# Attention segments with merged value tiles, a quarter of a normalisation on ScalarE, and scores between value projections

## The chip, the cores and the metric

One core of a Trainium2 chip. The metric is device time of one execution in microseconds; lower is better. TensorE (PE) does matmuls into PSUM, VectorE (DVE), ScalarE (ACT) and GpSimd (POOL) do the rest, and SyncE (SP) issues most DMAs. The kernel is one unrolled program; nothing is decided at run time.

## The reference

A transformer block on 2048 tokens of width 640. Only its first part matters here: a recurrent attention, 64 segments of 32 tokens, 32 heads of 128, with 8 memory tokens that each segment hands to the next.

```python
for s in range(n_seg):                      # 64
    xs = x[:, s * seg_len:(s + 1) * seg_len, :].copy()
    h = jnp.concatenate([mem, xs], axis=1)  # 8 + 32 tokens
    q = jnp.einsum('btd,dhe->bhte', h, Wq)  # k and v alike
    scores = jnp.einsum('bhqe,bhke->bhqk', q, k) * scale
    scores = jnp.where(mask[None, None], scores, -1000000000.0)
    p = _softmax(scores, axis=-1)
    o = jnp.einsum('bhqk,bhke->bhqe', p, v)
    o = jnp.einsum('bhte,hed->btd', o, Wo)
    mem = o[:, :M, :].copy()
    outs.append(o[:, M:, :])
```

x is layer-normalised before it. Behind it come a residual, a second layer norm and a gated ReLU feed-forward (640 to 1728 to 640), with a residual again.

## The kernel before, in words

All weights of the attention lie in SBUF. The program is a list of operations, written in one order; `_Graph` works out which semaphores each must wait for, and every engine runs its own operations in the order of the list. PSUM has eight banks, named `BQ` (0 and 1), `T0`, `T1` (2, 3) and `P0` to `P3` (4 to 7).

A segment's 40 tokens are split: 32 rows of `act_r` hold the memory and 24 tokens, and the last 8 tokens of four segments share one tile, `act_e`, whose keys, queries and values (`Ke`, `Qe`, `Ve`) are made once for four segments, in the group before. So each segment has two sets of keys and values: its own (`Ko`, `Vp`, index a = 0) and the shared ones (`Ke`, `Ve`, a = 1).

One turn of the loop over `s` does, on TensorE, in this order:

1. K projection of `act_r` in two halves of 16 heads (`project`, L374: five chunks of the width, four matmuls each side by side on column groups of 32, 512 columns). ScalarE evicts each half (`to_tok`, L395), VectorE transposes it in blocks of 32 (`flip`, L390) into `Ko`.
2. `pv_x(s-1)`: probabilities times values for the 32 new queries of the segment before, into banks 0 to 3, in tiles of 32 rows by 32 columns. `norm_x` divides by the row sum (a column of ones in the value tiles): one reciprocal (L648) and two products over 128x512 (L651) on VectorE, into `ox`; `flip_ox` (L535) transposes `ox` into `oT`.
3. Q projection in two halves, evicted and flipped as K, into `Qo`.
4. V projection half 0, `scores(s,0)`, V projection half 1, `scores(s,1)`. A call of `scores` is 32 matmuls (L460) with 40 columns. The values are evicted by ScalarE into `Vp` (two buffers, by the parity of s).
5. `pv_mem(s,0)`, a filler, `pv_mem(s,1)`, a filler: the 8 memory queries. Before each come `exp_mem` (ScalarE, into `Pm`) and `mask_mem` (VectorE, into `Pbd`); behind each `norm_mem` and `flip_mem` into `oT`. The fillers are parts of the shared projections (`extra_units`) or of the output projection of the shared tokens (`woe_pass`, L615).
6. `wo_split` (L572) and `wo_pass` (L555), the output projection. Its memory rows become, through `fold_split` and `to_act_split`, the first rows of the next `act_r`; the other rows go to DRAM from `wtok`.
7. The rest of the filler, while that runs; then the next segment.

`exp_x` and `mask_x` make the probabilities `Px` that the next turn's `pv_x` uses. SP also loads and transposes x for the segments to come (once in four segments).

Of the kernel before, what the change touches and what calls it, by code (L numbers as in the profile page):

```python
# [163 lines left out]
def build_kernel(nc, A_x, A_mem0, A_Wq, A_Wk, A_Wv, A_Wo, A_seg_len, B_W_gate, B_W_up, B_W_down, out):  # L164
# [57 lines left out]
    mca = ar.alloc("mca", [128, 5, SEG], BF16)  # L222
    act_r = [ar.alloc(f"act_r{i}", [128, 4, DC, 32], BF16) for i in range(2)]
    act_e = [ar.alloc(f"act_e{i}", [128, DC, 32], BF16) for i in range(2)]
    tok = [ar.alloc(f"tok{i}", [128, 512], BF16) for i in range(4)]
# [5 lines left out]
    Vp = [ar.alloc(f"Vp{i}", [128, 8, VW], BF16) for i in range(2)]  # L231
# [8 lines left out]
    ox = ar.alloc("ox", [128, 4, 2, Dh], BF16)  # L240
    wtok = [ar.alloc(f"wtok{i}", [128, DC, 32], BF16) for i in range(2)]
# [36 lines left out]
    for i in (1, 0):  # L278
        add("pool", lambda p, i=i: p.memset(wtok[i][:], 0.0), w=[("wtok", i)])
# [4 lines left out]
    for i in range(2):  # L284
# [3 lines left out]
        add("pool", lambda p, i=i: p.memset(ap(Vp[i], Dh, [[VW, 8], [1, VW - Dh]]), 1.0), w=[("Vp1", i)])  # L288
# [4 lines left out]
    for g in range(4):  # L293
        for n in range(5):
            sl = mca[32 * g:32 * g + 32, n, :]
            add("pool", lambda p, sl=sl, n=n: p.affine_select(sl, sl, [[1, SEG]], ALU.is_ge, 0.0,
                                                              base=M if n == 0 else M * (n - 1) - RID,
                                                              channel_multiplier=-1), r=[("mca",)], w=[("mca",)])
            if n > 1:
                add("pool", lambda p, sl=sl, n=n: p.affine_select(sl, sl, [[0, SEG]], ALU.is_ge, 0.0,  # L300
                                                                  base=-M * (n - 1), channel_multiplier=1),
                    r=[("mca",)], w=[("mca",)])
    add("pool", lambda p: p.memset(mbd[:], 0.0), w=[("mbd",)])
    for g in range(4):
        add("pool", lambda p, g=g: p.memset(mbd[32 * g:32 * g + 32, :, 8 * g:8 * g + 8], BIG), r=[("mbd",)], w=[("mbd",)])
# [73 lines left out]

    def to_tok(b, t, eng):  # L380
        copy_op(eng, tok[t][:, :], bank(b), [B(b)], [("tok", t)])
# [7 lines left out]
    def flip(t, dst, i, keys):  # L389
        add("dve", lambda v: v.transpose(dst[:, 16 * i:16 * i + 16, 0:32], tok[t][:, :].rearrange("p (h f) -> p h f", f=32)),  # L390
            r=[("tok", t)], w=keys)
# [58 lines left out]
    def scores(s, hf):  # L450
# [3 lines left out]
        def f(pe):  # L454
            for k in range(4 * hf, 4 * hf + 4):
                for a in range(2):
                    for g in range(4):
                        h = head(k, g)
                        o = 160 * a + 40 * (k % 4)
                        i = pe.matmul(bank((P0, P1)[hf])[32 * g:32 * g + 32, o:o + 40],  # L460
# [13 lines left out]
    def exp_mem(s, hf):  # L474
        _, j = place(s)
        add("act", lambda a: a.activation(ap(Pm, 32 * hf, [[64, 2], [8, 4], [1, 8]]), s_view(hf, 0, M), ACTF.Exp,
                                          scale=SCALE), r=[B((P0, P1)[hf])], w=[("Pm", hf)])

    def mask_mem(s, hf):
        _, j = place(s)  # L480
        for i in (1, 0):
            add("dve", lambda v, i=i: v.tensor_tensor(ap(Pbd, 256 * i + 128 * hf, [[32, 4], [8, 4], [1, 8]]),
                                                      ap(Pm, 64 * i + 32 * hf, [[8, 4], [0, 4], [1, 8]]),
                                                      ap(mbd, 32 * (1 + j) * i, [[0, 4], [8, 4], [1, 8]]), ALU.min),
# [7 lines left out]
    def mask_x(s):  # L492
# [3 lines left out]
                                             ap(mca, 0, [[32 * (1 + j), 2], [0, 8], [1, 32]]), ALU.min),  # L496
            r=[("Px", 0), ("Px", 1), ("mca",)], w=[("Px", 0), ("Px", 1)])

    def v_of(s, a):
        par, p = s % 2, place(s)[0]  # L500
        if a == 0:
            return Vp[par], [("Vp", par, i) for i in range(2)] + [("Vp1", par)]
        return Ve[p], [("Ve", p, i) for i in range(2)] + [("Ve1", p)]

    def pv_mem(s, hf):
# [10 lines left out]
        (vp, e), par = place(s), s % 2  # L516
        add("pe", f, r=[("Pbd", a, hf) for a in range(2)] + [("Ve", vp, hf), ("Ve1", vp), ("Vp", par, hf), ("Vp1", par)],
            w=[B(bk)])

    def norm_mem(s, hf):  # L520
# [3 lines left out]
        add("act", lambda a: a.activation(om[:, hf, :], src[:, 0:128], ACTF.Copy, scale=rm[:, hf:hf + 1]),  # L524
            r=[B(bk), ("rm", hf)], w=[("om", hf)])
# [6 lines left out]
    def flip_ox(s, halves=(0, 1)):  # L532
        p = (s + 1) % 2
        for kh in halves:
            add("dve", lambda v, kh=kh: v.transpose(ap(oT[p], 160 * kh + M, [[320, 4], [40, 4], [1, 32]]),  # L535
                                                       ap(ox, 128 * kh, [[256, 4], [1, 4], [4, 32]])),
                r=[("ox", kh)], w=[("oT", p, "x", kh)])
# [90 lines left out]

    def pv_x(s, b0):
        (t0, k0), (t1, k1) = v_of(s, 0), v_of(s, 1)  # L630

        def f(pe):
            for kh in range(2):
                for a in range(2):
                    for c in range(4):
                        k = 4 * kh + c
                        for g in range(4):
                            i = pe.matmul(bank(b0 + g)[32 * c:32 * c + 32, 129 * kh:129 * kh + 129],  # L638
                                          Px[32 * g:32 * g + 32, 256 * a + 32 * k:256 * a + 32 * k + 32],
                                          (t0, t1)[a][32 * g:32 * g + 32, k, 0:129], start=(a == 0), stop=(a == 1),  # L640
                                          skip_group_check=True, tile_position=(32 * g, 32 * c))
            return i
        add("pe", f, r=[("Px", 0), ("Px", 1)] + k0 + k1, w=[B(b0 + g) for g in range(4)])
# [254 lines left out]
    for s in range(1, NSEG):  # L898
# [16 lines left out]
        if s > 0:  # L915
# [24 lines left out]
            if s > 1:  # L940
                flip_ox(s - 1, (0,))
# [301 lines left out]
```

## Time and profile before

| | |
|---|---|
| median of 3 runs | 1027.08 us (1026.67 to 1027.17) |
| the profiled execution | 1026.84 us |
| its span | 1025.1 us |
| PE, PEld, DVE, ACT, POOL busy | 97%, 55%, 70%, 49%, 16% |
| granted TensorE clock | 0.998 |

A line of the page or the trace gives the line of the kernel, engine, operation and tiles; `x` is a count. In a timeline the first two numbers are start and length in microseconds from the start of the span, and a bracket at the end gives the engine's idle time before it and what ended that. PEld is TensorE's weight load, which overlaps its matmuls. A matmul's length holds its way through the array, so starts, not lengths, show the pace.

### The profile page before, as it was taken

To read this page: it belongs to the slowest core of one execution; us is meant where nothing else is said; L and a number is where in the kernel's file an instruction comes from. 1 tells how busy PE (TensorE), PEld (TensorE's weight loads), DVE (VectorE), ACT (ScalarE), POOL (GpSimd) and SP (SyncE) were. 2 spreads that over 40 slices of the span, in tenths; PEclk is the share of its full clock that TensorE was granted. 3 is DMA by queue.
4 is the path that set the end of the run, shared out by engine and by line. 5 is a ranking of instruction groups with operands and counts; after the bars stand their busy time and mean duration, and the time that the engine had idled before them with its cause. 6 is when DMAs were issued, how large, how long until landed. Compare 5 with 4: busy or idle time off the path is not lost.

```text
span 1025.1 us, 57915 instructions
## 1 busy us (share of the span) xinstructions
PE 994.6 (97%) x27201; PEld 559.5 (55%) x26104; DVE 716.0 (70%) x1796; ACT 501.5 (49%) x1262; POOL 168.8 (16%) x402
## 2 busy tenths in 40 slices
PE   4789999999999999999999999999999999999998
PEld 1255656565656565656565566656565554444443
DVE  2558787878778787888888778787777765355332
ACT  1345555555555555565556555555555542121220
POOL 6020202120202020222222222121210010000000
PEclk9999999999999999999999999999999999999999
DMA  9920100010001001111212111000000048413100
GB/s 372 416 68 6 21 7 21 7 22 7 21 7 22 7 21 12 29 18 23 46 27 32 28 32 22 20 8 16 9 6 8 8 114 242 130 27 90 27 14 26
DMA packets 58531, 52.23 MB, mean 51 GB/s; under 512 B 37840, under 2 KB 55216, under 8 KB 56368
## 3 DMA queue, kind: packets, MB, share of 16 engines
q1 hardware_dynamic: 56160, 47.23, 16.7%
q8 instruction: 208, 3.41, 1.4%
q10 hardware_dynamic: 2128, 1.31, 0.5%
q14 instruction: 35, 0.29, 0.1%
HBM read 37.04 MB, written 6.55 MB: 43 GB/s over the span
## 4 chain that ended last, share of the span: by engine, by line
PE 93%; SPq 3%; DMA 2%; issue 0%; DVE 0%; ACT 0%; DVEq 0%; ACTq 0%
PE ps L374 47%; PE ps L817 11%; PE ps L555 7%; PE ps L572 7%; PE ps L357 6%; PE ps L638 4%; PE ps L615 4%; SPq L320 3%; PE ps L1049 3%; PE ps L460 3%; DMA Wo<-in_A_Wo_dram 2%; PE ps L513 2%; PE ps L830 0%; PE ps L1061 0%; DVE TBf L595 0%
## 5 line engine op out<-in xcount | busy, mean ns | idle before, releaser
L374 PE MATMUL ps<-W,act_r 128*32 128x512 bf16 x7580 | 448.3, 381 | 2.1 <-DVE act_r L596 1.4
L374 PEld LDWEIGHTS ps<-W,act_r 128*32 128x32 bf16 x7580 | 190.6, 96 | 201.5 <-DVE act_r L596 31.2
L395 ACT ACTIVATE tok<-ps 128x512 bf16<-128x512 f32 x324 | 189.0, 597 | 163.5 <-PE ps L374 134.4
L374 PE MATMUL ps<-W,act_e 128*32 128x512 bf16 x1224 | 121.2, 383 | 7.5 <-DMA W<-in_A_Wv_dram 4.0
L468 POOL COPY Qo<-Qe 128x256 bf16<-128x256 bf16 x64 | 31.8, 497 | 547.4 <-DVE oT L529 524.4
L390 DVE STREAM_TRANSPOSE Ko<-tok 128x512 bf16<-128x512 bf16 x128 | 89.6, 701 | 40.0 <-ACT tok L395 36.9
L395 ACT ACTIVATE Vp<-ps 128x512 bf16<-128x512 f32 x127 | 75.8, 597 | 69.2 <-PE ps L374 69.2
L390 DVE STREAM_TRANSPOSE Qo<-tok 128x512 bf16<-128x512 bf16 x126 | 88.9, 706 | 14.1 <-ACT tok L395 14.1
L535 DVE STREAM_TRANSPOSE oT<-ox 128x512 bf16<-128x512 bf16 x128 | 87.8, 687 | 0.0
L357 PE MATMUL ps<-W,act_e 128*32 128x512 bf16 x856 | 87.7, 385 | 0.0
L555 PE MATMUL ps<-Wo,oT 128*32 128x160 bf16 x4032 | 83.3, 233 | 1.0 <-issue 0.6
L651 DVE TENSOR_TENSOR ox<-ps,rx 128x512 bf16<-128x512 f32 x128 | 82.5, 687 | 2.2
L572 PE MATMUL ps<-Wo,oT 128*32 128x320 bf16 x2016 | 81.2, 299 | 0.0
L555 PEld LDWEIGHTS ps<-Wo,oT 128*32 128x32 bf16 x4032 | 75.7, 97 | 5.8 <-DMA Wo<-in_A_Wo_dram 1.3
L585 ACT ACTIVATE SA<-TA 64x40 f32<-64x40 f32 x126 | 29.5, 234 | 84.9 <-DVE TA L583 84.2
L845 ACT ACTIVATE g<-ps 128x512 bf16<-128x512 f32 x52 | 30.1, 593 | 82.8 <-PE ps L817 82.8
L817 PE MATMUL ps<-xn2T,Wu 128*128 128x512 bf16 x260 | 64.6, 379 | 0.0
L846 DVE TENSOR_TENSOR hT<-g,ps 128x512 bf16<-128x512 bf16 x52 | 35.8, 688 | 40.5 <-PE ps L817 40.1
L572 PEld LDWEIGHTS ps<-Wo,oT 128*32 128x32 bf16 x2016 | 56.4, 96 | 13.8 <-issue 1.1
L374 PEld LDWEIGHTS ps<-W,act_e 128*32 128x32 bf16 x1224 | 37.1, 97 | 47.8 <-issue 34.8
L817 PE MATMUL ps<-xn2T,Wg 128*128 128x512 bf16 x246 | 61.6, 379 | 1.5 <-issue 1.1
L529 DVE STREAM_TRANSPOSE oT<-om 128x128 bf16<-128x128 bf16 x126 | 39.2, 311 | 29.4 <-ACT om L524 28.1
(109 smaller groups left out, 1359.1 us busy)
## 6 DMA issues: line engine op xcount, KB each, us to landing
W<-in_A_Wk_dram SPq DMA_DIRECT2D x5, 1024.0 KB
W<-in_A_Wq_dram SPq DMA_DIRECT2D x5, 1024.0 KB
W<-in_A_Wv_dram SPq DMA_DIRECT2D x5, 1024.0 KB
Wo<-in_A_Wo_dram SPq DMA_DIRECT2D x8, 640.0 KB
attn_d<-wtok SPq DMA_DIRECT2D x248, 7.5 KB
xt<-in_A_x_dram SPq DMA_DIRECT2D x16, 160.0 KB
at<-attn_d SPq DMA_DIRECT2D x16, 160.0 KB
out_dram<-osb SPq DMA_DIRECT2D x15, 160.0 KB
```

The costliest lines, as they stand in the source:

```text
L357: return pe.add_instruction(mybir.InstMatmult(name=nc.get_next_instruction_name(), engine=mybir.EngineType.PE, ins=[pe.lower_ap(rhs), pe.l ...
L374: ins = pe.matmul(*a, start=(c == 0), stop=(c == DC - 1), skip_group_check=True)
L390: add("dve", lambda v: v.transpose(dst[:, 16 * i:16 * i + 16, 0:32], tok[t][:, :].rearrange("p (h f) -> p h f", f=32)), r=[("tok", t)], w= ...
L395: add("act", lambda a: a.activation(dst, src, ACTF.Copy), r=r, w=w)
L529: add("dve", lambda v: v.transpose(ap(oT[par], 160 * hf, [[40, 4], [320, 4], [1, 8]]), ap(om, 128 * hf, [[1, 4], [4, 32]])), r=[("om", hf) ...
L535: add("dve", lambda v, kh=kh: v.transpose(ap(oT[p], 160 * kh + M, [[320, 4], [40, 4], [1, 32]]), ap(ox, 128 * kh, [[256, 4], [1, 4], [4, 3 ...
L555: i = pe.matmul(bank(bk)[32 * gg:32 * gg + 32, 0:160], src[:, hb, 0:32], w[:, gg], start=(hb == CH[16 * halves[0]]), stop=(hb == CH[-1]), ...
L572: i = pe.matmul(bank(bk)[32 * q:32 * q + 32, 0:320], src[:, hb, 0:32], w, start=(n == 0), stop=(n == 7), skip_group_check=True)
L615: ins = pe.matmul(bank(bk)[32 * q:32 * q + 32, 0:320], src[:, hb, 0:32], w[:, 2 * (q % 2):2 * (q % 2) + 2], start=(i == 0), stop=(i == 15) ...
L638: i = pe.matmul(bank(b0 + g)[32 * c:32 * c + 32, 129 * kh:129 * kh + 129], Px[32 * g:32 * g + 32, 256 * a + 32 * k:256 * a + 32 * k + 32], ...
L651: add("dve", lambda v, kh=kh: v.tensor_tensor(ox[:, :, kh, :], src[:, :, kh, 0:128], ap(rx, kh, [[2, 4], [0, 128]]), ALU.mult), r=[B(b0 + ...
L817: ins = pe.matmul(bank(bk), w[:, c, lo:lo + 128], xn2T[par][:, c, :], start=(c == 0), stop=(c == DC - 1))
```

## The change

- The scores of the two key sets are written so that partitions 64u to 64u + 63 hold, for one head, the probabilities of both sets. To match, the shared values are projected with neighbouring head groups swapped, and `merge_v` copies `Vp` and `Ve` by DMA from SP into two merged value tiles `VM`: four copies of 32 partitions per segment, and four more once in four segments. `pv_x` then needs 32 matmuls on tiles of 64 rows by 32 columns instead of 64 on 32 by 32, without accumulation. `Vp` and `wtok` lose a buffer; `ox` shares memory with two of the `tok` tiles (`tox`).
- `norm_x` does the reciprocal and the first half of the product on VectorE. `norm_x_late`, after the eviction and flip of the first Q half, does the rest: a quarter on VectorE, a quarter on ScalarE in two pieces.
- Scores come in runs of 16 matmuls: after four of the five chunks of a value half, and after the fifth.
- `exp_mem(s,0)` and `exp_mem(s,1)` stand ahead of the evictions of the value halves. `norm_mem(s,0)` scales on VectorE instead of ScalarE.
- `pv_x(0)` moves from the start into the turn s = 1.

```diff
+    tox = ar.alloc("tox", [128, 4, 2, Dh], BF16)
+    tok = [tox[:].rearrange("p g k d -> p (g k d)")[:, 512 * i:512 * i + 512] for i in range(2)]
...
-    Vp = [ar.alloc(f"Vp{i}", [128, 8, VW], BF16) for i in range(2)]
+    Vp = ar.alloc("Vp", [128, 8, VW], BF16)
+    VM = [ar.alloc(f"VM{i}", [128, 8, VW], BF16) for i in range(2)]
...
     def project(act, akeys, j, halves, banks, chunks=range(5)):
+        swap = 1 if j == 2 and akeys[0][0] == "acte" else 0
...
-                        w = (W[:, j, c, o + 512 * g:o + 512 * g + 512] if j == 2 else
+                        w = (W[:, j, c, o + 512 * (g ^ swap):o + 512 * (g ^ swap) + 512] if j == 2 else
...
-    def scores(s, hf):
+    def scores(s, hf, ks=range(4)):
...
-            for k in range(4 * hf, 4 * hf + 4):
+            for k in [4 * hf + n for n in ks]:
                 for a in range(2):
                     for g in range(4):
                         h = head(k, g)
-                        o = 160 * a + 40 * (k % 4)
-                        i = pe.matmul(bank((P0, P1)[hf])[32 * g:32 * g + 32, o:o + 40],
+                        o, q = 160 * (g % 2) + 40 * (k % 4), 32 * (g ^ a)
+                        i = pe.matmul(bank((P0, P1)[hf])[q:q + 32, o:o + 40],
...
-        add("act", lambda a: a.activation(om[:, hf, :], src[:, 0:128], ACTF.Copy, scale=rm[:, hf:hf + 1]),
-            r=[B(bk), ("rm", hf)], w=[("om", hf)])
+        if hf:
+            add("act", lambda a: a.activation(om[:, hf, :], src[:, 0:128], ACTF.Copy, scale=rm[:, hf:hf + 1]),
+                r=[B(bk), ("rm", hf)], w=[("om", hf)])
+        else:
+            add("dve", lambda v: v.tensor_scalar(om[:, hf, :], src[:, 0:128], rm[:, hf:hf + 1], None, ALU.mult),
+                r=[B(bk), ("rm", hf)], w=[("om", hf)])
...
+    def merge_v(s, a):
+        (t, ks), flat = v_of(s, a), "p k d -> p (k d)"
+        for r in range(2):
+            for g in range(4):
+                if g % 2 == r ^ a:
+                    dma(VM[r][32 * g:32 * g + 32].rearrange(flat), t[32 * g:32 * g + 32].rearrange(flat), r=ks,
+                        w=[("VM", r, g)])
+
     def pv_x(s, b0):
...
-                for a in range(2):
+                for r in range(2):
                     for c in range(4):
                         k = 4 * kh + c
-                        for g in range(4):
-                            i = pe.matmul(bank(b0 + g)[32 * c:32 * c + 32, 129 * kh:129 * kh + 129],
-                                          Px[32 * g:32 * g + 32, 256 * a + 32 * k:256 * a + 32 * k + 32],
-                                          (t0, t1)[a][32 * g:32 * g + 32, k, 0:129], start=(a == 0), stop=(a == 1),
-                                          skip_group_check=True, tile_position=(32 * g, 32 * c))
+                        for u in range(2):
+                            i = pe.matmul(bank(b0 + 2 * u + r)[32 * c:32 * c + 32, 129 * kh:129 * kh + 129],
+                                          Px[64 * u:64 * u + 64, 256 * r + 32 * k:256 * r + 32 * k + 32],
+                                          VM[r][64 * u:64 * u + 64, k, 0:129], start=True, stop=True,
+                                          skip_group_check=True, tile_position=(64 * u, 32 * c))
...
+    def norm_x_late(b0):
+        src = ps[:, b0 * 512 + 1024:b0 * 512 + 2048].rearrange("p (g r) -> p g r", r=512)[:, :, 129:257]
+        add("dve", lambda v: v.tensor_tensor(tox[:, 2:4, 1, :], src, ap(rx, 5, [[2, 2], [0, 128]]), ALU.mult),
+            r=[B(b0 + 2), B(b0 + 3), ("rx",)], w=[("ox", 1, 1)])
+        for g in range(2):
+            add("act", lambda a, g=g: a.activation(tox[:, g, 1, :], bank(b0 + g)[:, 129:257], ACTF.Copy,
+                                                   scale=rx[:, 2 * g + 1:2 * g + 2]),
+                r=[B(b0 + g), ("rx",)], w=[("ox", 1, 0)])
...
-            if s > 1:
-                pv_x(s - 1, 0)
-                norm_x(0)
+            pv_x(s - 1, 0)
+            norm_x(0)
+            if s % 4 == 2:
+                merge_v(s, 1)
             if not last:
                 for i in range(2):
                     project(a, ks, 0, (i,), ((P0, P1)[i],))
                     to_tok((P0, P1)[i], 2 + i, "act")
                     flip(2 + i, Qo, i, [("Qo", i)])
-            if s > 1:
+                    if i == 0:
+                        norm_x_late(0)
+                        flip_ox(s - 1, (0,))
...
-            project(a, ks, 2, (0,), (P2,))
-            to_v(P2, Vp[par], 0, ("Vp", par), "act")
+            project(a, ks, 2, (0,), (P2,), range(4))
+            scores(s, 0, (0, 1))
+            project(a, ks, 2, (0,), (P2,), (4,))
+            scores(s, 0, (2, 3))
+            if not last:
+                exp_mem(s, 0)
+                mask_mem(s, 0)
+            to_v(P2, Vp, 0, ("Vp",), "act")
...
-        exp_mem(s, 0)
-        mask_mem(s, 0)
-        if s > 0:
-            if s > 1:
-                flip_ox(s - 1, (1,))
-            to_v(P3, Vp[par], 1, ("Vp", par), "act")
+        project(a, ks, 2, (1,), (P3,), range(4))
+        scores(s, 1, (0, 1))
+        project(a, ks, 2, (1,), (P3,), (4,))
+        scores(s, 1, (2, 3))
+        flip_ox(s - 1, (1,))
...
         exp_mem(s, 1)
+        to_v(P3, Vp, 1, ("Vp",), "act")
+        merge_v(s, 0)
         pv_mem(s, 0)
```

The masks (`mbd`, `mca`) and the layouts of `Pm` and `Pbd` follow the new places of the scores.

More of the change, by code (lines that the diff above doesn't have):

```diff
@@ L239, in build_kernel @@
     rx = ar.alloc("rx", [128, 8], F32)
-    ox = ar.alloc("ox", [128, 4, 2, Dh], BF16)
-    wtok = [ar.alloc(f"wtok{i}", [128, DC, 32], BF16) for i in range(2)]
+    wtok = ar.alloc("wtok", [128, DC, 32], BF16)
     TBf = ar.alloc("TBf", [128, DC, 32], F32)
@@ L275, in B @@
         return ("B", n)
-    for i in (1, 0):
-        add("pool", lambda p, i=i: p.memset(wtok[i][:], 0.0), w=[("wtok", i)])
+    add("pool", lambda p: p.memset(wtok[:], 0.0), w=[("wtok",)])
     add("pool", lambda p: p.memset(ident[:], 1.0), w=[("ident",)])
@@ L378, in project, with tok_keys @@
         add("pe", f, r=list(akeys) + [("W", j, c) for c in chunks], w=[B(b) for b in banks] + [("Wdone", j)])
+    def tok_keys(t):
+        return [("tok", t)] + [("ox", kh, t) for kh in range(2) if t < 2]
     def to_tok(b, t, eng):
-        copy_op(eng, tok[t][:, :], bank(b), [B(b)], [("tok", t)])
+        copy_op(eng, tok[t][:, :], bank(b), [B(b)], tok_keys(t))
     def to_v(b, t, i, key, eng):
@@ L515, in f @@
             return i
-        (vp, e), par = place(s), s % 2
-        add("pe", f, r=[("Pbd", a, hf) for a in range(2)] + [("Ve", vp, hf), ("Ve1", vp), ("Vp", par, hf), ("Vp1", par)],
+        vp = place(s)[0]
+        add("pe", f, r=[("Pbd", a, hf) for a in range(2)] + [("Ve", vp, hf), ("Ve1", vp), ("Vp", hf), ("Vp1",)],
             w=[B(bk)])
@@ L709, in build_kernel @@
     w0 = bank(T1)[:, 0:160]
-    copy_op("dve", w0, wtok[1][:].rearrange("p c t -> p (c t)"), [("wtok", 1)] + [("wtok0", g) for g in range(4)],
+    copy_op("dve", w0, wtok[:].rearrange("p c t -> p (c t)"), [("wtok",)] + [("wtok0", g) for g in range(4)],
             [B(T1), ("w0",)])
@@ L872, in build_kernel @@
     pv_mem(0, 1)
-    pv_x(0, P0)
+    for a in (1, 0):
+        merge_v(0, a)
     for hf in range(2):
@@ L963, in build_kernel @@
             gate_up(0, 0)
-        scores(s, 1)
-        if last:
+            scores(s, 1)
             exp_x(s, 1)
@@ L1132, in build_kernel @@
     norm_x(P0)
+    norm_x_late(P0)
     flip_ox(s)
```

89 lines of the change are left out of this document (45 added, 44 removed).

## The prediction

> **What bounds it now.** I read the page first, then the list of TensorE's waits, then TensorE's timeline through one segment, then VectorE's and ScalarE's over the same stretch, and last the records of DMA packets. The page:
>
> ```profile
> PE 994.6 (97%) x27201; PEld 559.5 (55%) x26104; DVE 716.0 (70%) x1796; ACT 501.5 (49%) x1262; POOL 168.8 (16%) x402
> PEclk9999999999999999999999999999999999999999
> PE 93%; SPq 3%; DMA 2%; issue 0%; DVE 0%; ACT 0%; DVEq 0%; ACTq 0%
> ```
>
> TensorE is busy 97% at full clock and carries 93% of the chain that ends last. Its list of waits:
>
> ```profile
> PE ps L374 <- DVE act_r L596: 1.4, 2, 0.8
> PE ps L513 <- DVE Pbd L482: 0.8, 1, 0.8
> ```
>
> These are the largest that lie inside the 64 segments (the longer ones are in the start). So only a shorter TensorE stream can shorten this kernel, and only if nothing it waits for becomes late. One segment takes 12.40 us (three in four; the fourth, with the load of x, 12.5 to 13.0). Where is TensorE busy but badly used?
>
> ```profile
> 406.72 0.82 PE L374 MATMUL ps<-W,act_r 128*32 128x512 bf16 x12
> 407.47 0.28 PE L638 MATMUL ps<-Vp,Px 32*32 32x129 bf16 x16
> 407.54 0.28 PE L638 MATMUL ps<-Ve,Px 32*32 32x129 bf16 x16
> 407.72 0.35 PE L638 MATMUL ps<-Vp,Px 32*32 32x129 bf16 x16
> 407.86 0.35 PE L638 MATMUL ps<-Ve,Px 32*32 32x129 bf16 x16
> 408.13 0.61 PE L374 MATMUL ps<-W,act_r 128*32 128x512 bf16 x8
> ```
>
> This is `pv_x`. Four 512-column matmuls side by side take 0.2165 us in the projections (60 in 3.25 us), so 129 columns stream in 0.054 us, and four rounds of 16 tiles could take 0.22 us. The rounds start at 0, 0.07, 0.25 and 0.39 us, and the next projection at 0.665. The first two rounds are 64 instructions (weight loads and matmuls); from there each pair comes 8.3 ns after the last, the pace at which instructions arrive, not stream. After the last matmul's start another 0.157 us pass before the projection.
>
> ```profile
> 411.38 0.19 PE L460 MATMUL ps<-Qo,Ko 128*32 128x40 bf16 x4
> 411.41 0.19 PE L460 MATMUL ps<-Qo,Ke 128*32 128x40 bf16 x4
> ...
> 411.54 0.19 PE L460 MATMUL ps<-Qo,Ko 128*32 128x40 bf16 x4
> 411.57 0.23 PE L460 MATMUL ps<-Qo,Ke 128*32 128x40 bf16 x4
> 411.63 1.28 PE L374 MATMUL ps<-W,act_r 128*32 128x512 bf16 x20
> ```
>
> A half of the scores: groups of four start 25.5 ns apart while instructions are at hand, and the last groups are spread out; 32 matmuls cost 0.25 us.
>
> **Part by part.** *pv_x, 32 matmuls on 64-row tiles instead of 64.* Its 64 instructions are what the fast stretch held. Entry and exit stay (still two changes of tile shape). Four rounds of 8 tiles: the last matmul starts at 0.03 + 3 x (0.054 to 0.071) = 0.19 to 0.24, plus 0.157 out: 0.35 to 0.40 against 0.665, a gain of 0.27 to 0.32; I take 0.29. The loop and the tail have 63 that were on the path: -18.3 us. No row has a 64-row tile; if the two row halves did not run side by side, eight rounds would leave a gain of about 0.04, the other bound. The Trainium skill ("TensorEngine Tiling (Array Packing)", Tiling Modes) lists 64x32 as eight independent tiles, which would be the first bound; no run here shows it.
>
> *pv_x(0) moves* from the start, where it lay under the load of Wo (the chain has 20.13 us of that from 35.40), into segment 1: about +0.5 us.
>
> *Scores in runs of 16.* Two halves now cost 0.25 each, with 0.007 more in the projection behind. A run of 16 is 32 instructions, so it never runs dry: four steps of 25.5 ns, 0.10 us, four runs per segment. But the order of the column groups is now 0,1,2,3,1,0,3,2, so a group returns after three matmuls instead of four; at 3.5 ns between matmuls this adds up to 0.014 per run. Gain 0.05 to 0.10, and nothing if each added entry costs another 0.015; I take 0.07 x 62 = -4.3 us.
>
> *Merge DMAs.* Four per segment (eight in one of four) on SP, 66 KB each, 32 rows of 2080 bytes. They wait for the second value eviction, which ends about 0.9 us after the start of `pv_mem(s,0)`, and are issued at about 0.4 us each (four stores of `wtok` took 1.51), done by 2.6. The 160 KB load of x began to move 1.0 us after its issue and its last row landed, behind an instruction fetch, at 3.0. So they land 4 to 5.6 us after `pv_mem(s,0)`; `pv_x` comes 6.9 us after it. Queued behind them on SP are the `wtok` stores, whose next writer comes a segment later, and behind the four that wait for `pv_x` only the next merge, 5 us on; so they cost nothing. If they landed 2 us later still, that cover would be gone and each further microsecond would cost 62.
>
> *Their packets against instruction fetches.* TensorE's program comes in 16384-byte blocks, 0.92 to 1.0 us each usually, up to 1.8 while x is loading; then the `wo` passes sometimes stop without a semaphore (0.47 us at 167.2, 0.56 at 565.8). Those passes use 128 instructions in 1.1 us. The merge puts about two rows per engine and DMA there, against eight for x. Bounds 0 and 0.5 us per segment; only blocks fetched in the 1.1 us before those passes matter, so I take the low end, +1 us in all. The Trainium skill ("Runtime: NRT & Kernel Launch", Instruction fetch mechanics) says that TensorE holds 2048 instructions and that crossing a block is mostly hidden. By that rule this term would be 0 and the total 1 us lower; the two stops speak against it.
>
> *Waits on TensorE.* `pv_x` now waits for four DMA semaphores. A semaphore instruction on TensorE takes 0.051 us, two follow 0.11 apart (929.32), and matmuls already queued went on at their 0.136 step beside them; here the 64 instructions ahead are 1.7 us of projection. So 0; if they were exposed, 0.22 x 62 = 14 us. `pv_mem(s,0)` now waits for ScalarE too: the first value eviction, after `exp_mem(s,0)`, ends about 0.3 us before it is wanted.
>
> *VectorE and ScalarE.* Here the cover is thin.
>
> ```profile
> 408.22 0.71 DVE L390 STREAM_TRANSPOSE Ko<-tok 128x512 bf16<-128x512 bf16 x1 [0.37 <-ACT tok L395]
> 408.86 0.17 DVE L648 RECIPROCAL rx<-ps 128x8 f32<-128x8 f32 x1
> 409.06 1.29 DVE L651 TENSOR_TENSOR ox<-ps,rx 128x512 bf16<-128x512 f32 x2
> 410.26 0.70 DVE L390 STREAM_TRANSPOSE Qo<-tok 128x512 bf16<-128x512 bf16 x1
> 411.16 0.71 DVE L390 STREAM_TRANSPOSE Qo<-tok 128x512 bf16<-128x512 bf16 x1 [0.19 <-ACT tok L395]
> ```
>
> Count from the first load of `pv_x` (407.47). The reciprocal stays at 1.39, the first half of the normalisation at 1.59; the first Qo flip follows at 2.28 (its eviction comes 0.29 earlier than now). `norm_x_late` on VectorE, 256 elements from PSUM: 0.32 us for 160 (L602) and 0.69 for 512 bound it, about 0.42 on their line; it starts at 2.91. `flip_ox` at 3.25, and the second Qo flip, formerly third, at 3.85, done at 4.56, visible to TensorE at 4.61. TensorE wants it for the second half of the scores at 0.375 + 2.165 (Q) + 0.866 + 0.105 + 0.2165 + 0.105 + 0.866 = 4.70. It is 0.09 us early, where before it was 0.8 early. ScalarE's two pieces (0.37 each, L524's shape) fit between the two Qo evictions, which leave 0.48 idle plus the earlier start. Behind it, `exp_mem(s,1)` now precedes the value eviction (0.27 earlier), `om(0)` on VectorE (128 elements, about 0.29) replaces a ScalarE step and its semaphore, and Pbd's second half comes 1.08 after `pv_mem(s,0)`, as now; TensorE asks for it at 1.13. So two covers under 0.1 us: I add +1 us for segments that miss them.
>
> **Sum.** -18.3 + 0.5 - 4.3 + 1 + 1 = -20.1. The profiled execution took 1026.84 (span 1025.10 and 1.74 around it), 0.24 below the median of 1027.08: 1006.7, and 1007.0 for the median.
>
> **Rivals.** (1) *VectorE becomes the bound.* If `norm_x_late` takes a full-size 0.69 instead of 0.42, the second Qo flip is 0.18 late in every segment: 62 x 0.18 = 11, 1017 with the 1 us above taken out. For it: 9 to 10.3 us busy of 12.4 per segment, with no idle from 1.39 on. Against: the operand is half as large. (2) *64-row tiles run one half at a time*: +0.25 x 63 = 16, 1023. For it: no row; against: 4 x 4 tiles of 32 rows do run together. (3) *The other side: fetches behind the merge.* If every segment stops for the 0.47 us seen at 167.2, 62 x 0.47 = 29, 1035 with the 1 us taken out. It decides from 0.34 us per segment, where the gain is gone. For it: the merge falls into the `wo` passes each time; against: 1/4 of x's rows per DMA. (4) *The change doesn't do its work faster*, since exit and entry, not arrival, set 0.665: excluded by the 8.3 ns pace of the last 32 pairs. (5) *More than I take*: rounds at 0.054 and runs at 0.10 throughout, no stops: 63 x 0.03 + 62 x 0.03 + 2 = 6 less, 1001.
>
> **Numbers.** Forecast 0.60 (1003 to 1012), more than taken 0.12 (998 to 1003), VectorE 0.13 (1012 to 1020), half tiles 0.06 (1020 to 1025), fetches 0.06, and 0.03 for the cases in which half tiles or fetches end within 0.2% of 1027.1 (about what a measurement can tell from no change). Faster 0.60 + 0.12 + 0.13 + 0.06 = 0.91, less 0.01 for half tiles that miss it; same 0.03; slower 0.07. The range leaves out half tiles and slower, and the top of VectorE: 999 to 1018.
>
> **What would show it.** `pv_x` of 32 matmuls with the next projection 0.35 to 0.40 us after its first; four runs of scores at 0.10 to 0.12; segments of 12.0 to 12.1 us; in TensorE's waits nothing above 2 us for Qo, Pbd or VM. I am wrong if Qo or VM heads that list, if `pv_x` shows rounds 0.11 apart, or if the `wo` passes stop without a semaphore in most segments.

## The result: 1012.7 us, 1.4% less

| | before | after |
|---|---|---|
| median (lowest to highest) | 1027.1 us (1026.67 to 1027.17) | 1012.74 us (1011.48 to 1013.14) |
| ratio | | 0.9858, 95% interval 0.9843 to 0.9872 |
| profiled execution, span | 1026.84, 1025.1 us | 1012.37, 1009.9 us |

The forecast was 1007.0 us within 999 to 1018: right direction, inside the range, and 5 to 6 us too much gain. The page of the kernel after:

```profile
PE 973.2 (96%) x25153; PEld 513.8 (51%) x24056; DVE 712.7 (71%) x1859; ACT 520.3 (52%) x1327; POOL 167.4 (17%) x416
PEclk9999999999999999999999999999999999999999
PE 92%; SPq 3%; DMA 3%; DVE 1%; issue 1%; ACT 0%; POOL 0%; DVEq 0%; ACTq 0%
```

TensorE lost 2048 matmuls and stays the bound at the same clock, but VectorE has entered the chain with 1%. `pv_x` in TensorE's timeline:

```profile
484.56 0.82 PE L380 MATMUL ps<-W,act_r 128*32 128x512 bf16 x12
485.31 0.42 PE L658 MATMUL ps<-VM,Px 64*32 64x129 bf16 x32
485.66 0.83 PE L380 MATMUL ps<-W,act_r 128*32 128x512 bf16 x12
```

The next projection starts 0.351 us after the first matmul, where it was 0.665. In the single records the four rounds of eight tiles start at 485.305, .373, .430 and .487, 0.06 to 0.07 us apart: the two row halves do run side by side. The scores of one half, same view:

```profile
136.81 0.19 PE L469 MATMUL ps<-Qo,Ko 128*32 128x40 bf16 x4
...
136.91 0.39 PE L380 MATMUL ps<-W,act_r 128*32 128x512 bf16 x4
137.13 0.19 PE L469 MATMUL ps<-Qo,Ko 128*32 128x40 bf16 x4
```

A run of 16 takes 0.10 us and then the projection goes on.

This is one regular segment (turn 31, s = 31) on TensorE, by the starts of its blocks in both traces:

| block | before | after | difference |
|---|---|---|---|
| `pv_x` to the next projection | 0.663 | 0.351 | -0.312 |
| scores of the first half, of the second half | 0.249, 0.251 | 0.204, 0.205 | -0.091 |
| steps behind them (V half 1, first `pv_mem`) | | | -0.021 |
| second `pv_mem`, with its wait | 0.329 | 0.376 | +0.047 |
| all else | | | -0.004 |
| the segment | 12.404 | 12.023 | -0.38 |

So the steady gain is 0.38 per segment, 23.2 us over the 61 segments from `pv_x(1)` to `pv_x(62)`; the forecast had 0.36. The span fell by 15.2: +1.1 until `pv_x(1)`, -14.8 over those 61, -0.35 to `pv_x(63)`, -1.2 behind it. Thus 8.4 us came back inside the loop. Sorted by s % 4, the time above 61 regular segments (12.40 and 12.02) is

| s % 4 | 0 | 1 | 2 | 3 |
|---|---|---|---|---|
| before | 0.1 | 4.2 | 0.6 | 0.1 |
| after | 5.2 | 6.2 | 2.0 | 0.1 |

The largest piece, 4.5 us, lies in three turns: 36 (13.23 us), 40 (14.80) and 44 (12.51). In a second profile of the same kernel (last experiment) they take 13.36, 12.86 and 12.79, 2.9 us above the regular one. There GpSimd adds attention to x for an early second normalisation (`add_attn`, L690 after, L662 before). Its row among the groups of instructions (busy time and mean ns, then GpSimd's idle time before it and what ended that), of the kernel before and then of the kernel after:

```profile
L662 POOL TENSOR_TENSOR xt<-xt,at 128x640 bf16<-128x640 bf16 x4 | 5.6, 1398 | 16.7 <-DVE Ko L390 16.7
```

```profile
L690 POOL TENSOR_TENSOR xt<-xt,at 128x640 bf16<-128x640 bf16 x4 | 5.8, 1461 | 30.6 <-DMA at<-attn_d 26.4 <-DVE Ko L399 4.2
```

Before, it started with the Ko flip at the head of the turn. After, it waits for a load. SP's timeline of the kernel after says why (turns 35 and 36; `pv_x` of turn 36 starts at 485.31):

```profile
479.96 1.87 SPq L325 DMA_DIRECT2D VM<-Vp  x3
481.88 2.19 SPq L348 DMA_TRANSPOSE at<-xt  x1
...
488.77 0.34 SPq L325 DMA_DIRECT2D at<-attn_d  x1
...
493.03 2.46 SPq L325 DMA_DIRECT2D VM<-Vp  x4
```

The merges of turn 35 stand ahead of the transpose of xt, and a chain of waits on SP (transpose, store, load) follows, so `at` is asked for only at 488.77, 3.5 us into turn 36. What that late addition meets, over all engines:

```profile
491.16 1.40 POOL L690 TENSOR_TENSOR xt<-xt,at 128x640 bf16<-128x640 bf16 x1 [8.48 <-DMA at<-attn_d]
491.21 1.56 DVE L491 TENSOR_TENSOR Pbd<-Pm,mbd 128x128 bf16<-128x128 bf16 x2
...
492.83 0.24 PE L522 MATMUL ps<-Ve,Pbd 128*32 128x129 bf16 x4 [1.08 <-DVE Pbd L491]
```

The first of VectorE's two masks takes 1.424 us instead of 0.22; it ends 0.08 us after GpSimd's addition. TensorE waits 1.08 us for it. In turn 44 the same mask takes 0.70 us and TensorE waits 0.35. Turn 40, the longest of the three, holds up no mask. There the addition comes later still, and GpSimd's own next steps stand behind it; the next `act_r` needs them, and TensorE waits 1.14 us:

```profile
542.60 1.65 POOL L690 TENSOR_TENSOR xt<-xt,at 128x640 bf16<-128x640 bf16 x1 [10.18 <-DMA at<-attn_d]
...
545.80 0.20 DVE L609 TENSOR_TENSOR act_r<-TBf,SA 128x40 bf16<-128x40 f32 x1 [1.34 <-POOL SA L600]
...
546.06 0.40 PE L380 MATMUL ps<-W,act_r 128*32 128x512 bf16 x4 [1.14 <-DVE act_r L609]
```

SP, in turn, holds the next merges behind `h_d<-xt`, which waits for the addition; in turn 40 they land so late that `pv_x` itself waits. TensorE's list has the wait for the mask (with 0.9 us that lies elsewhere) and the wait for the merges:

```profile
PE ps L522 <- DVE Pbd L491: 2.4, 3, 1.1
PE ps L658 <- DMA VM<-Vp: 1.4, 1, 1.4
```

**Theory 1**: the missing gain went into these turns, through SP's order and two engines that shut each other out. **Theory 2**: it is the merges' packets, which slow instruction fetches and land late in any turn. **Theory 3**: the terms of the sum are mis-sized.

### The profile page after: what moved, and what is told of

It is laid out like the page before. It is cut to its first block, busy times and chain, and to the rows that moved or that the text cites. A ratio compares the mean times of both kernels' runs of the same rounds, so it can differ in the third digit from the quotient of the medians.

```text
span 1009.9 us, 54668 instructions
## 1 busy us (share of the span) xinstructions
PE 973.2 (96%) x25153; PEld 513.8 (51%) x24056; DVE 712.7 (71%) x1859; ACT 520.3 (52%) x1327; POOL 167.4 (17%) x416
## 4 chain that ended last, share of the span: by engine, by line
PE 92%; SPq 3%; DMA 3%; DVE 1%; issue 1%; ACT 0%; POOL 0%; DVEq 0%; ACTq 0%
PE ps L380 47%; PE ps L845 11%; PE ps L568 7%; PE ps L585 6%; PE ps L362 6%; PE ps L628 4%; SPq L325 3%; PE ps L1086 3%; PE ps L469 2%; PE ps L658 2%; DMA Wo<-in_A_Wo_dram 2%; PE ps L522 2%; DMA VM<-Vp 1%; PE ps L858 0%; PE ps L1098 0%
## 5 line engine op out<-in xcount | busy, mean ns | idle before, releaser
L380 PE MATMUL ps<-W,act_r 128*32 128x512 bf16 x7580 | 455.3, 380 | 3.8 <-DVE act_r L609 2.2
L404 ACT ACTIVATE tok<-ps 128x512 bf16<-128x512 f32 x190 | 109.3, 594 | 59.9 <-PE ps L380 51.3
L380 PE MATMUL ps<-W,act_e 128*32 128x512 bf16 x1224 | 120.1, 384 | 7.7 <-DMA W<-in_A_Wv_dram 4.0
L399 DVE STREAM_TRANSPOSE Ko<-tox 128x512 bf16<-128x512 bf16 x128 | 89.7, 702 | 41.8 <-ACT tox L404 41.1
L477 POOL COPY Qo<-Qe 128x256 bf16<-128x256 bf16 x64 | 27.8, 434 | 522.6 <-DVE oT L542 492.3
L404 ACT ACTIVATE tox<-ps 128x512 bf16<-128x512 f32 x134 | 79.6, 598 | 58.3 <-PE ps L380 36.8
L548 DVE STREAM_TRANSPOSE oT<-tox 128x512 bf16<-128x512 bf16 x128 | 89.6, 700 | 0.0
L362 PE MATMUL ps<-W,act_e 128*32 128x512 bf16 x856 | 84.9, 386 | 0.0
L568 PEld LDWEIGHTS ps<-Wo,oT 128*32 128x32 bf16 x4032 | 72.0, 97 | 12.8 <-DMA Wo<-in_A_Wo_dram 3.9
L485 ACT ACTIVATE Pm<-ps 128x64 bf16<-128x64 f32 x126 | 28.1, 223 | 70.1 <-PE ps L469 70.0
L585 PEld LDWEIGHTS ps<-Wo,oT 128*32 128x32 bf16 x2016 | 54.0, 96 | 16.6 <-DVE rm L532 1.2
L469 PE MATMUL ps<-Qo,Ko 128*32 128x40 bf16 x2048 | 61.2, 180 | 0.0
```

The costliest lines, as they stand in the source:

```text
L362: return pe.add_instruction(mybir.InstMatmult(name=nc.get_next_instruction_name(), engine=mybir.EngineType.PE, ins=[pe.lower_ap(rhs), pe.l ...
L380: ins = pe.matmul(*a, start=(c == 0), stop=(c == DC - 1), skip_group_check=True)
L404: add("act", lambda a: a.activation(dst, src, ACTF.Copy), r=r, w=w)
L469: i = pe.matmul(bank((P0, P1)[hf])[q:q + 32, o:o + 40], (Ko if a == 0 else Ke[p])[:, h, :], Qo[:, h, :], start=True, stop=True, skip_group ...
L568: i = pe.matmul(bank(bk)[32 * gg:32 * gg + 32, 0:160], src[:, hb, 0:32], w[:, gg], start=(hb == CH[16 * halves[0]]), stop=(hb == CH[-1]), ...
L585: i = pe.matmul(bank(bk)[32 * q:32 * q + 32, 0:320], src[:, hb, 0:32], w, start=(n == 0), stop=(n == 7), skip_group_check=True)
```

## Experiments

Each was timed against the kernel before on its chip; ratios are to that kernel. Differences between versions are those of their medians. The changed kernel itself came out at 1012.74 and, in the last experiment, at 1014.27 us, so a difference under 2 us between two versions says little by itself.

### SP's transfers ahead of the merges

```diff
+        if e2c is not None:                       # head of the turn
+            flip_rows(chunks_of(at[:, :]), xt, ("xt",), ("at",))
+            dma(xn2_d[...], chunks_of(at[:, :]), ...)
+        if s % 4 == 3 and e2 is not None:
+            dma(xt[:, :], x_ap[...], w=[("xt",)])
+            load_attn(at, e2, [], ("at",))
...                                               # and gone from their old places
```

> The changed kernel with four transfers of the early normalisation (the transpose of xt into at, the store of xn2_d, the loads of xt and at) put ahead of the segment's merges on SP, at the head of turns 31, 35, 39, 43 and 47. Theory 1 (the missing 5 us went into turns 36, 40 and 44: SP reaches these transfers late because the merges stand before them, so GpSimd's addition runs beside VectorE's mask and holds it up, and SP, waiting for that addition, issues the next merges late): turns 36, 40 and 44 return to 12.0 to 12.1 us, GpSimd's addition starts within 0.2 us of the Ko flip as in the kernel before, and the time falls by 3.5 to 4.5 us to 1008.2 to 1009.2. Theory 2 (the missing time is the merges' packets themselves, which slow instruction fetches and land late in any turn): within 0.5 us of the changed kernel's 1012.7.

Measured: 1012.09 us (1011.39 to 1014.26), ratio 0.9859 (0.9846 to 0.9871): hardly a gain, and by the time alone theory 2 comes closer. Yet the turns did what theory 1 says: GpSimd's addition waits only for Ko again (17.0 us over four), and the s % 4 = 0 turns fell from 5.2 to 0.4 us above the regular one. The s % 4 = 3 turns rose from 0.1 to 2.1: turns 35, 39, 43 and 47 took 12.38 to 12.71. The 61 segments became 3.2 us shorter; 1.0 us ahead of `pv_x(1)` and 2.0 behind `pv_x(62)` took that back, and no run shows why. SP in turn 35 of this kernel (it starts at 474.07, the next `pv_x` at 486.45):

```profile
473.99 1.23 SPq L348 DMA_TRANSPOSE at<-xt  x1
...
479.95 0.34 SPq L325 DMA_DIRECT2D at<-attn_d  x1
480.40 3.20 SPq L325 DMA_DIRECT2D VM<-Vp  x4
```

Now the merges are behind the chain of waits. Their last issue begins at 483.01, it lands 3.35 us later, and the first weight load of `pv_x` starts 0.06 us after that. In these turns SP could not have both the chain and the merges done in time.

### The additions on VectorE

```diff
-            if s % 4 == 0 and e2 is not None:
-                add_attn(xt[:, :], xt, at, [("xt",), ("at",), ("Ko", 1)], [("xt",)], "pool")
-                dma(h_d[...], xt[:, :], ...)
...
         if s % 4 == 0 and e2 is not None:         # end of the turn
+            add_attn(xt[:, :], xt, at, [("xt",), ("at",)], [("xt",)])
+            dma(h_d[...], xt[:, :], ...)
             row_moments(xt, ("xt",), 128)
```

> The changed kernel with the four early additions of attention to x moved from GpSimd, beside the first mask, to VectorE at the end of the turn (h_d is stored after it); SP's order is not touched otherwise. Theory 1: no mask is stretched any more (0.18 to 0.21 us each) and no merge waits for the addition, so turns 36, 40 and 44 lose their 4.5 us, less up to 0.5 us for four additions of 0.48 us on VectorE: 1008.2 to 1009.2. If only the lateness of SP mattered and not the two engines' meeting, turn 36 keeps its 1.2 us and turn 40 part of its 2.8: 1010.5 to 1012. Theory 2: within 0.5 us of 1012.7.

Measured: 1009.6 us (1008.06 to 1010.34), ratio 0.9829 (0.9816 to 0.9842), 3.1 us below the changed kernel. The s % 4 = 0 turns fell to 0.8 us above the regular one (4.4 less), with SP's merges and loads in the same order (only the store of `h_d` moved); TensorE's wait for Pbd fell from 2.4 to 0.9 us, and no wait for VM is left among its ten largest. Theory 1 holds: the late additions made these turns long. This run takes away the held masks, GpSimd's lateness in turn 40 and the late merges at once; the experiment after the next has the first of them alone. Part of the 4.4 went elsewhere: the s % 4 = 2 turns rose by 1.3.

### No merges

```diff
-        merge_v(s, 0)            # and merge_v(s, 1); only those of segment 0 are left
```

> The changed kernel without its merges from segment 1 on: VM keeps the values of segment 0, so the attention over x is computed with old values; all else is as it was. It gives the whole price of the merges. Theory 1: 4 to 5 us back (1007.7 to 1008.7), all of it in turns 36, 40 and 44; TensorE's stops without a semaphore in the turns with a load of x stay as they are. Theory 2: 8 us or more back (1004.7 or less), with the stops in the turns with a load of x gone too and no waits for VM.

Measured: 1009.03 us (1008.64 to 1011.68), ratio 0.9833 (0.982 to 0.9846): 3.7 us back, near theory 1's 4 to 5 and far from theory 2's 8. Against the kernel with the additions on VectorE that is 0.6 us, inside both intervals. In the profiles the 61 segments are 5.8 us shorter, 4.8 of it in the s % 4 = 0 turns, and 2.5 us are lost behind `pv_x(63)`, which no run explains. The s % 4 = 1 turns keep 5.75 of their 6.15 us, so what makes those long is not the merges.

Outside the three turns the merges do show, but little. `pv_x` usually starts 0.31 us after the matmuls before it. In the changed kernel the one that ends turns 8, 38, 45 and 58 starts 0.13 to 0.28 us later than that, each time 0.09 us after the last of its merges has landed; without the merges no turn has such a step. That is 0.9 us in all (in the second profile 1.5, in five turns). The list of waits has it in part as "issue", as at the end of turn 38:

```profile
523.02 0.42 PE L658 MATMUL ps<-VM,Px 64*32 64x129 bf16 x32 [0.20 <-issue]
```

### The lock by itself

```diff
         norm_mem(s, 0)
+        if s % 4 == 3:
+            add("pool", lambda p, ...: p.tensor_tensor(scr..., one, one, ALU.add),
+                r=[("rm", 0), ("ident",)], w=[("TA",)])
```

> The kernel with the four early additions on VectorE (1009.6 us), plus one GpSimd addition of 128x640 (both operands from SBUF, its result in a buffer that is dead then) in each of the 15 turns with s%4 = 3, set free by the first reciprocal of norm_mem, so that it runs when VectorE wants to mask the second half of the scores. Nothing waits for its result except GpSimd's next step, later in the turn. If the two engines' operations shut each other out (theory 1): the mask lasts until GpSimd is done, 1.2 to 1.4 us in place of 0.18, and TensorE waits about 1.1 us for Pbd in each: 15 to 18 us more, 1024 to 1028. If the 1.4 us mask of turn 36 was late data or chance: 1009 to 1011.

Measured: 1023.11 us (1020.74 to 1025.51), 13.5 above the kernel without it. Turn 31 over three engines:

```profile
436.43 1.25 POOL L1018 TENSOR_TENSOR TA<-ident 128x640 bf16<-128x640 bf16 x1 [8.31 <-DVE rm L532]
436.65 1.24 DVE L491 TENSOR_TENSOR Pbd<-Pm,mbd 128x128 bf16<-128x128 bf16 x2
...
437.95 0.24 PE L522 MATMUL ps<-Ve,Pbd 128*32 128x129 bf16 x4 [0.75 <-DVE Pbd L491]
```

Again the first mask ends with GpSimd's operation (1.11 us instead of 0.22). Nearly every s % 4 = 3 turn takes 12.91 instead of 12.02: 15 x 0.89 = 13.4 us. I had expected 1.1 each; this addition took 1.25 us and started earlier, so less of it was exposed. The product `om` next to it, which reads PSUM, kept its 0.35 us. The Trainium skill ("SBUF — State Buffer", Who interferes with whom) states just this: a VectorE instruction with two inputs in SBUF and a GpSimd instruction that reads SBUF exclude each other, and whichever comes second is blocked until the first has finished. The trace agrees, 1.424 and 1.11 us for a mask of 0.22; in turn 40 it went the other way, GpSimd's 1.40 became 1.65 beside `mask_x`.

### The scores in full runs again

```diff
-        project(a, ks, 2, (1,), (P3,), range(4))
-        scores(s, 1, (0, 1))
-        project(a, ks, 2, (1,), (P3,), (4,))
-        scores(s, 1, (2, 3))
+        project(a, ks, 2, (1,), (P3,))             # half 0 alike
+        scores(s, 1)
```

> The changed kernel with each half's scores in one run of 32 behind the whole value projection again, instead of two runs of 16 with a chunk of the projection between. The prediction's term for the runs was 0.07 us per segment, 4.3 us in all; the segment's measured gain less that of pv_x (0.375 less 0.314) leaves 0.061, 3.8 us. So 1016.2 to 1017.3, with a regular segment of 12.08 to 12.10. If the runs gained nothing and the segment's rest came from elsewhere (the order of the exponentials), the time stays within 0.5 us of 1012.7.

Measured: 1026.4 us (1021.56 to 1027.96), ratio 0.9984 (0.9972 to 0.9995). Undoing this part costs 13.7 us, over three times my term. A regular segment grows by 0.125 to 12.146: 0.03 in the first half, 0.10 in the second, where `pv_mem` starts 0.11 us after the last scores:

```profile
138.38 0.21 PE L469 MATMUL ps<-Qo,Ke 128*32 128x40 bf16 x4
138.49 0.24 PE L522 MATMUL ps<-Ve,Pbd 128*32 128x129 bf16 x4
```

An instruction that waits on a semaphore takes 0.051 us of TensorE's queue there and now lies bare; after a run of 16 the same step takes 0.025. That makes 61 x 0.125 = 7.6 us. The other 6 lie in single turns and behind the loop. Stops without a semaphore, which the list of waits calls "issue", are a part of them. Over all lines they make 7.1 us here, 2.4 and 4.7 in the two profiles of the changed kernel, and 3.1 in the kernel before. One profile of each version can't say how much of the difference is the version's.

### Full runs without merges

The edits of "No merges" and of "The scores in full runs again" together.

> The experiment with the scores in full runs (1026.4 us), without its merges from segment 1 on; VM keeps the values of segment 0. It tells what made TensorE stop without a semaphore for 7.1 us in that kernel. If the merges' packets delay the instruction fetches (the prediction's third rival): the stops fall to 2 or 3 us, as in the changed kernel without merges, and the time to 1009.0 plus 7.7 for the longer segment, 1016 to 1018. If the stops come from where the blocks end in the stream and not from other packets: the stops stay at 5 us or more, and the time falls only by the 3.7 us that the merges cost in the changed kernel, 1021.5 to 1024.

Measured: 1018.88 us (1017.71 to 1021.48), ratio 0.9916 (0.9903 to 0.993), between the two expectations. By the medians the merges cost 7.5 us in this kernel and 3.7 in the changed one. That merges make the stops longer is not shown: the profile, of the slowest run (1021.48), still has 5.5 us of stops with no merge in sight, against 7.1 with them, and in the profiles the 61 segments lose 5.7 us with the merges here and 5.8 in the changed kernel. What decides how many stops a kernel has is not settled by these runs.

### pv_x in 64 matmuls again

```diff
-                        for u in range(2):
-                            i = pe.matmul(bank(b0 + 2 * u + r)..., Px[64 * u:64 * u + 64, ...], VM[r][64 * u:64 * u + 64, ...])
+                        for g in range(4):
+                            i = pe.matmul(bank(b0 + g)..., Px[32 * g:32 * g + 32, ...], VM[r][32 * g:32 * g + 32, ...])
```

> The changed kernel with pv_x in 64 matmuls of 32 rows again, on the same tiles, banks and order as before, reading the merged values; its sums over r pair other values than the attention's, so only its time counts. The prediction's term of 0.29 us per segment, measured as 0.31, gives 18.3 to 19.8 us on the changed kernel's 1012.7: 1031 to 1032.5. If the block's length came from its entry and exit, or if part of the segment's gain came from elsewhere, less than 1025.

Measured: 1040.22 us (1039.42 to 1042.15), ratio 1.0132 (1.0119 to 1.0145): 27.5 more. The regular segment went from 12.02 to 12.33 (+0.313, all between `pv_x` and the next projection), 63 x 0.313 = 19.7 us as expected. The other 8 us lie in single turns, and again come with stops: 7.6 us of "issue" on the list of waits, where the changed kernel's two profiles have 2.4 and 4.7.

### The x normalisation on VectorE alone

```diff
-        add("dve", ... tox[:, 2:4, 1, :] ...)      # and two pieces on ScalarE
+        add("dve", lambda v: v.tensor_tensor(tox[:, :, 1, :], src, ap(rx, 1, [[2, 4], [0, 128]]), ALU.mult), ...)
```

> The changed kernel with the whole second half of the x normalisation on VectorE (512 elements from PSUM, about 0.69 us) and none of it on ScalarE. By the prediction's schedule the second Qo flip has 0.09 us to spare, so 0.3 us more on VectorE ahead of it costs about 0.2 us in each of 62 segments, 13 us: 1024 to 1027, with waits for Qo at the scores. If the cover is wider than the prediction made it, the time stays within 1 us of 1012.7.

Measured: 1022.73 us (1021.53 to 1026.05), ratio 0.9963 (0.9949 to 0.9976), 10 more; the regular segment 12.215, 0.19 more. The operation on VectorE took 0.65 us (0.385 in the changed kernel) and the second half of the scores moved from 4.663 to 4.846 us after `pv_x`. VectorE's and TensorE's timelines of turn 31 in this kernel:

```profile
435.33 0.67 DVE L399 STREAM_TRANSPOSE Qo<-tok 128x512 bf16<-128x512 bf16 x1
...
436.06 0.20 PE L469 MATMUL ps<-Qo,Ko 128*32 128x40 bf16 x4
```

The scores start 0.06 us after the flip's end. The prediction's 0.09 us of spare cover was right to 0.02: 0.27 more work, 0.18 more time.

### The runs of scores and the exponentials in the kernel before

The same lines as in the diff of the change for `scores`, `exp_mem` and the value evictions, and nothing else.

> The kernel before with two parts of the change alone: each half's scores in two runs of 16 with a chunk of the value projection between, and the exponentials of the memory part ahead of the value evictions. pv_x, the values and the normalisation of x are as before. The prediction's term is 4.3 us and the traces leave 3.8: 1022.8 to 1023.4. If the runs are worth in this kernel what undoing them cost in the changed one (13.7 us), 1013 to 1014; if most of that cost was instruction fetches that met the merges, 1022 to 1024.

Measured: 1042.73 us (1040.65 to 1044.08), ratio 1.0152 (1.0137 to 1.0166): 16 us slower than the kernel before, against every expectation. The runs do what they should (0.205 us per half instead of 0.25), but `wo_split` then starts 0.474 us after the matmuls ahead of it instead of 0.216, and the usual segment is 12.55. The row of `flip_mem` in this kernel:

```profile
L529 DVE STREAM_TRANSPOSE oT<-om 128x128 bf16<-128x128 bf16 x126 | 39.5, 313 | 61.5 <-ACT om L524 61.5
```

VectorE's idle time before it doubled (28.1 us behind `om` in the kernel before): with the exponential ahead, the value eviction (0.59 us) stands right before `om` on ScalarE, so the flips come late. The changed kernel scales `om(0)` on VectorE; without that part, the order of the exponentials costs more than the runs bring. This is read from the timeline; no run has the runs of scores here without that order. The longer segments make some 7 of the 16 us. The rest lies in single turns, where stops grew from 0.6 us in the loop to 5.3, without any merge.

### Masks ahead of om(0)

```diff
     def norm_mem(s, hf, between=None):
         ... reciprocal ...
+        if between:
+            between()                              # mask_mem(s, 1) for hf = 0
         ... om ...
```

> The changed kernel with the two masks of the scores' second half put between the reciprocal and the product of norm_mem(s,0) on VectorE, ahead of om(0). In the changed kernel's regular segment the second pv_mem starts 0.252 us after the matmuls before it where 0.216 is their own step, so TensorE waits 0.036 us for Pbd, and 0.1 us in every fourth segment. If that wait is VectorE's order: the steps go and the segment falls to 11.98, 2.3 to 4 us in all: 1008.7 to 1010.4. If it is something else (ScalarE's exponential, the semaphore's own cost): 1012.2 to 1013.

Measured: 1012.7 us (1011.95 to 1013.37), ratio 0.9855 (0.9841 to 0.9868); the changed kernel in the same rounds took 1014.27. The wait went: the second `pv_mem` starts 0.216 us after the matmuls before it. But `wo_split` now waits, and the segment gained 0.018, not 0.05. The rows of the weight loads (busy and mean, then idle time before them), of the changed kernel and then of this one:

```profile
L522 PEld LDWEIGHTS ps<-Ve,Pbd 128*32 128x32 bf16 x504 | 13.0, 93 | 25.7 <-DVE Pbd L491 24.2 <-DVE Ve L406 1.5
```

```profile
L522 PEld LDWEIGHTS ps<-Ve,Pbd 128*32 128x32 bf16 x504 | 14.7, 93 | 15.1 <-DVE Pbd L491 13.6 <-DVE Ve L406 1.5
L587 PEld LDWEIGHTS ps<-Wo,oT 128*32 128x32 bf16 x2016 | 48.5, 96 | 24.5 <-DVE oT L544 11.3 <-DVE rm L532 1.2 <-issue 0.9
```

The idle time behind Pbd fell by 10.6 us, and 11.3 behind oT are new: VectorE is the bound in this stretch, and another order of its work moves most of the wait elsewhere.

### Both gains, and the changed kernel again

> Both edits that gained: the four early additions on VectorE and the masks ahead of om(0). If the two causes are separate, their gains add: 1009.6 less 2.3 to 4 is 1005.6 to 1007.3, below both kernels. If the masks' earlier place only moves VectorE's lateness to the flips behind it (as in the experiment that put the runs of scores into the kernel before), 1009 to 1011.

> The changed kernel once more, on the same chip and in the same rounds as the three others, for their comparison: 1012.7, within 0.7 us, by every theory.

Measured: 1009.37 us (1008.38 to 1011.61), ratio 0.9826 (0.9812 to 0.984), beside 1014.27 (1013.64 to 1015.03), ratio 0.987 (0.9857 to 0.9884), for the changed kernel. The version with the additions on VectorE beats both kernels, by 3 to 5 us and 18 us; the masks' place adds nothing to it.

## Why the prediction was right, and where it missed

- **pv_x, -18.3**: right. 0.312 per segment for 0.29, 19.7 us; undone, it cost 0.313. The rival of half tiles fell with the rounds 0.06 us apart.
- **Scores, -4.3**: too small. The two halves and the steps behind them gave 0.112 per segment, 6.9 us. I counted the runs and took off a penalty for the order of the column groups that doesn't show: each run of 16 took 0.10. The 2.6 us above my figure hid as much of what I missed elsewhere, which was luck.
- **VectorE's covers, +1**: right in place, too small in size. The cover of the second Qo flip was 0.09 us as worked out (the normalisation on VectorE alone cost what that leaves). The other one, Pbd's second half, was not met: 0.047 per segment, 2.9 us. I had it 1.08 us after the start of `pv_mem(s,0)`; it came at 1.17, because `om(0)` on VectorE took 0.35 us for my 0.29 and the masks behind it are that much later. Together with the scores' term the segment came out at 0.38 for 0.36.
- **Merge DMAs, 0**: the step that failed. I took 0.4 us per issue from the stores of `wtok`; a merge takes 0.59. They landed 1.9 us (shortest), 2.1 (median) and 3.6 (nine in ten below) after issue, typically 1.1 us before `pv_x`, where I had 1.3 to 2.9. So the cover I took for safe ran out in four turns outside the three, for 0.9 us. The larger miss is that I asked only what is queued behind them in a regular segment, the stores, and not in the turns where SP carries the early normalisation's chain. There they made a GpSimd operation late. It met VectorE's masks (1.4 us of waits on TensorE, turns 36 and 44), held up GpSimd's own next steps (1.1, turn 40) and kept the next merges late (1.4, turn 40). In all the three turns lost 4.5 us, 2.9 in the second profile.
- **Fetches, +1**: about right in size, though no run shows that the merges' packets are the cause. Between `pv_x(1)` and `pv_x(62)`, without those that are waits for a merge, the stops grew from 0.6 us to 1.1 in the first profile of the changed kernel and to 3.0 in the second. They are larger in neighbours of this kernel (7.1 us over all lines with full runs, 7.6 with 64 matmuls), so forecasting them at 1 was luck as much as reason. The rule of the Trainium skill weighed there, that crossing a block is mostly hidden, holds by count: with full runs, 13 stops stand against 193 blocks of 16384 bytes. But a crossing that isn't hidden cost 0.2 to 1.0 us there.
- **pv_x(0), +0.5**: +1.1 until `pv_x(1)`, in the changed kernel's two profiles 0.9 and 1.1.

In sum 23.2 us of steady gain (forecast 22.6 before the +1 for covers), 8.4 back in irregular turns (forecast 1, for fetches), and the two ends about even. Of the 8.4, the three turns are 4.5 and the other late merges 0.9. The remaining 3, mostly in turns with s % 4 = 1 and 2, are open: most of that is there without the merges too, and the stops cover only a part.

## What to carry to other kernels

Before a DMA is put on a queue, list what stands behind it in every kind of turn, the rare ones too, and follow each to the engine it makes late. When a step moves in time, ask which operation of another engine it will then run beside. And don't price the parts of a change one by one if one pays for another: here the runs of scores and the earlier exponentials alone made the kernel before 16 us slower, and undoing the runs made the new one 13.7 us slower.

## What the runs showed of the hardware

- VectorE's mask with both inputs in SBUF (0.18 to 0.22 us) was held until GpSimd's addition ended, 1.424 us at the longest.
- A copy from SBUF to SBUF of 32 rows of 2080 bytes took 0.59 us of SP per issue (median) and 1.9 to 3.6 us to its semaphore for nine in ten. Of the 324 in the changed kernel's first profile, 94 took over 3 us; in 79 of these a 16384-byte block of TensorE's program was moving between 1.0 and 1.9 us after the issue, but only in 51 of the 172 that took under 2.3. So a late merge mostly had an instruction fetch beside it. This is read from the packet records; no run tested it.
- A stop without a semaphore ended 1.3 to 1.6 us after the last packet of the instruction block before it: 141.51 to 142.90 and 154.95 to 156.37 (full runs), 551.90 to 553.30 and 165.55 to 167.13 (no merges), 334.63 to 336.00 and 625.37 to 626.69 (the kernel before with runs of scores). Over all such stops in the loop in these traces it is 1.1 to 1.6. So it seems that a block whose packets have landed is not yet at hand. This is read from the packet records and TensorE's starts; no run tested it.
